# Reordering the prologue of a fused attention and token-mixer kernel, moving layernorm products to GpSimd, and telling its scheduler when the PV bank comes free

## Chip, cores and metric

The kernel runs on 1 core of one Trainium2 chip. The metric is the device time of one execution in microseconds (us); times are medians of 4 to 8 runs (two for `after_filler`, one for `forms`). A profile is one profiled execution, and its span is about 2 us shorter than its time. The engines are PE (TensorE; PEld is its weight load), ACT (ScalarE), DVE (VectorE), POOL (GpSimd) and SP (SyncE), which issues most DMAs here.

A ratio is of one kernel's runs to the other's of the same rounds. It is not the ratio of the medians quoted beside it, and differs from it by up to 0.15%. Different rounds ran on different chips; across rounds, the ratios compare better than the times.

## The reference

```
x = A_x                                   # 1 x 2048 x 512, bf16
xn = layernorm(x)                         # over the last axis, no weights
# A: attention, 32 heads of 16
q, k, v = split(xn @ wqkv)
oA = softmax(q k^T / 4) v  @ wo
# B: MLP over the token axis
h = layernorm(xn)
u = gelu(einsum("bsd,sf->bdf", h, w1) + b1)           # f = 1376
oB = transpose(einsum("bdf,fs->bds", u, w2) + b2)
out = x + oA + oB
```

## The kernel before

All instructions are generated by a Python program. For each engine it keeps a modelled clock and gives each instruction a cost. A prologue and attention block 0 (16 periods of two score tiles each) have a fixed order. The other 31 blocks are ordered by a greedy scheduler: at each step it takes the candidate that its model says can start first. Each engine gets its own list in that order; semaphores carry the dependences. So nothing on the chip waits for a modelled time; it decides the order.

A score tile of 128x1024 is exponentiated by ACT, or by DVE in a form of its own ("dexp", followed by three shifts on DVE or POOL). By the page of this kernel one took 1.14 to 1.15 us on ACT (L640), a dexp 1.22 us on DVE (L651), and a shift 0.45 us on DVE or 1.05 us on POOL (L656), all means. There are 1024 such tiles, called exps below, 32 to a block. "PV" is the product of probabilities and V, collected in one PSUM bank for a whole block. At the block's end DVE copies that bank out into OT.

The parts that matter:

```python
# prologue: memsets on POOL, the last of them
sc.add("pool", lambda e: e.memset(wo_t[:], 0.0), writes=[("wo_t", z) for z in range(4)], cost=(0.5, 0.6))
...
def late_consts():                    # called after block 0
    ... dma("sp", wo_c[...], ...)     # 8 loads
    ... dma("sp", wo_t[...], ...)     # 4 loads, after the wo_t memset
...
def ln_stats(t):                      # DVE bn_stats, bn_aggr; then POOL: (var + eps) ** -0.5
    ...
def ln_norm(t):
    sc.add("dve", lambda e: e.tensor_scalar(xn_sb[:, t, :], x_sb[:, t, :], mv[:, t, 0:1], mv[:, t, 2:3],
                                            ALU.subtract, ALU.mult), ...)
...
def pro_stage(s_, pre):               # one stage of the pipeline; period p of block 0 is stage p + 6
    # s_-5: evacuate K and V;  s_-4: K, (Q), V matmuls;  s_-3: copy xnT;  s_-2: transposes
    t = s_
    if ...: ln_stats(t)               # statistics first,
    t = s_ - 1
    if ...: ln_norm(t)                # then the product of the tile before it
...
for period in range(NKT):             # block 0
    # two score tiles and their exps on ACT; from period 2 on PV of two earlier ones
    block0_work(period)
late_consts()
for ft in range(NW): w1_load(ft)
...
# in the scheduler: PV is offered when its inputs are ready
jobs.append((max(t_c, a[0]), 0 if low else 2, "pv", a[1], 0.107))
```

The softmax here doesn't subtract the row's maximum and nothing guards it: scores larger than these inputs give would overflow.

## Time and profile before

| | before |
|---|---|
| time, median of 4 | 749.58 us (749.19 to 751.36) |
| ACT / PE / DVE / POOL busy | 95% / 92% / 86% / 47% |
| end of the 1st, 32nd, 1024th exp | 16.5, 47.9, 732.9 us |
| from the 32nd exp to the end of the span | 702.5 us |
| exps on DVE | 266 of 1024 |
| TensorE clock at half | 48.7 us of the span |

The exp times are the ends of exp instructions of the trace, put in order over ACT and DVE. The half-clock time is the sum of the clock's records in the trace, cut at the end of the span.

Three lines of the page: busy time by engine, and ACT and the granted TensorE clock in 40 slices of the span, in tenths.

```profile
PE 691.1 (92%) x12388; PEld 306.2 (41%) x12388; DVE 644.6 (86%) x1061; ACT 710.8 (95%) x779; POOL 351.5 (47%) x391
...
ACT  4899999999999999999999999989989999999990
...
PEclk9899999999999999999999999978989999999897
```

ACT is at 8 or 9 tenths from the second slice to the last but one, so time is to be had where ACT waits: at the start, and where the clock dips. The timeline of the start (start us, duration us, engine, line, operation, count, and in brackets the idle time before and what ended it):

```profile
4.16 1.80 POOL L400 MEMSET wo_t<- 128x2048 bf16 x1
...
6.04 0.23 POOL L456 TENSOR_SCALAR mv<-mv 128x1 f32<-128x1 f32 x1
...
6.35 0.57 POOL L458 TENSOR_TENSOR mv<-mv,mhalf 128x1 f32<-128x1 f32 x1
...
6.96 0.41 DVE L462 TENSOR_SCALAR hx<-x_sb,mv 128x512 bf16<-128x512 bf16 x1 [1.85 <-POOL mv L458]
...
14.25 0.69 ACT L553 ACTIVATE QT<-ps,qmask 128x512 bf16<-128x512 f32 x1 [0.60 <-PE ps L547]
...
15.43 5.75 ACT L640 ACTIVATE pT<-ps 128x1024 bf16<-128x1024 f32 x6 [0.32 <-PE ps L616]
```

POOL's memsets hold up the first rstd, and with it the first layernorm product (L462). The first exp starts at 15.43 us.

The waits over the span (who waited for whom: us in total, times, longest):

```profile
DVE pT L651 <- PE ps L616: 41.4, 50, 2.9
...
DVE x_sb L651 <- PE ps L616: 15.4, 17, 3.4
...
PE ps L679 <- DVE OT L863: 13.3, 26, 1.3
ACT pT L640 <- PE ps L616: 9.7, 15, 1.3
```

PE waits 26 times for the PV bank to be copied out; DVE waits 57 us for scores to exponentiate, and ACT 9.7. A line of the groups in the first 40 us (busy us, mean ns of one):

```profile
L531 POOL TENSOR_SCALAR VM<-V 128x544 bf16<-128x544 bf16 x3 | 1.9, 649 | 0.3
```

This is V times a constant, of about the product's size, in 0.65 us.

### The profile page before, as it was taken

How to read it: one execution, taken by the hardware profiler on the slowest of the kernel's cores; microseconds unless marked ns; L12 is line 12 of the kernel's file. 1: busy time of each engine (PE TensorE's matmuls, PEld its weight loads, DVE VectorE, ACT ScalarE, POOL GpSimd, SP SyncE). 2: the span in 40 equal slices, each digit the busy share in tenths (PEclk: the TensorE clock that was granted, in tenths of full speed). 3: DMA queues.
4: the chain of work that ended last, by engine and by line, in shares of the span. 5: the costliest groups of instructions: out<-in, count | busy, mean ns of one | idle time of the engine just before them, and what ended most of it. 6: DMA issues, size and time to landing. Idle time of an engine off the chain costs nothing.

```text
span 750.4 us, 28208 instructions
## 1 busy us (share of the span) xinstructions
PE 691.1 (92%) x12388; PEld 306.2 (41%) x12388; DVE 644.6 (86%) x1061; ACT 710.8 (95%) x779; POOL 351.5 (47%) x391
## 2 busy tenths in 40 slices
PE   4989999999999999999889999989899999989995
PEld 3544444444444434443333444333333444434332
DVE  6857788988999898899889988987979989999885
ACT  4899999999999999999999999989989999999990
POOL 6448355533434244355545435453454536446451
PEclk9899999999999999999999999978989999999897
DMA  7400000133233222210001222100001122111020
GB/s 206 84 3 24 18 13 17 23 73 72 47 69 65 62 49 51 54 43 21 23 15 31 50 51 61 36 15 16 23 16 29 47 51 52 38 31 36 17 58 29
DMA packets 85691, 32.25 MB, mean 43 GB/s; under 512 B 67392, under 2 KB 85568, under 8 KB 85568
## 3 DMA queue, kind: packets, MB, share of 16 engines
q1 hardware_dynamic: 82400, 28.87, 16.6%
q8 instruction: 97, 1.59, 0.9%
q10 hardware_dynamic: 3168, 1.57, 0.7%
q14 instruction: 26, 0.21, 0.1%
HBM read 21.76 MB, written 2.35 MB: 32 GB/s over the span
## 4 chain that ended last, share of the span: by engine, by line
ACT 41%; PE 31%; DVE 20%; POOL 3%; issue 2%; SPq 2%; DMA 0%; DVEq 0%; POOLq 0%
ACT pT L640 29%; PE ps L679 13%; ACT x_sb L640 12%; PE ps L616 11%; DVE pT L651 7%; PE ps L709 7%; DVE pT L656 5%; DVE x_sb L651 3%; SPq L371 2%; DVE OT L863 2%; DVE x_sb L656 1%; POOL pT L656 1%; POOL x_sb L656 1%; PE ps L758 1%; DVE denb L928 0%
## 5 line engine op out<-in xcount | busy, mean ns | idle before, releaser
L640 ACT ACTIVATE pT<-ps 128x1024 bf16<-128x1024 f32 x529 | 527.2, 1142 | 10.4 <-PE ps L616 9.7
L616 PE MATMUL ps<-QT,KT 32*128 32x512 bf16 x2048 | 285.1, 392 | 19.3 <-ACT pT L640 9.2
L651 DVE TENSOR_SCALAR pT<-ps 128x1024 int16<-128x1024 f32 x197 | 240.4, 1220 | 42.7 <-PE ps L616 41.4
L679 PE MATMUL ps<-pT,V 128*32 128x256 bf16 x4456 | 243.7, 282 | 13.6 <-DVE OT L863 7.0
L640 ACT ACTIVATE x_sb<-ps 128x1024 bf16<-128x1024 f32 x229 | 248.4, 1153 | 1.9 <-PE ps L616 1.9
L656 POOL TENSOR_SCALAR pT<-pT 128x1024 int16<-128x1024 int16 x137 | 143.5, 1047 | 175.6 <-DVE pT L656 125.1
L616 PEld LDWEIGHTS ps<-QT,KT 32*128 32x128 bf16 x2048 | 78.0, 91 | 194.4 <-ACT pT L640 80.7
L679 PEld LDWEIGHTS ps<-pT,V 128*32 128x32 bf16 x4456 | 106.0, 97 | 115.1 <-issue 72.5
L679 PE MATMUL ps<-x_sb,V 128*32 128x256 bf16 x1768 | 117.5, 282 | 9.0 <-DVE OT L863 6.3
L656 DVE TENSOR_SCALAR pT<-pT 128x1024 int16<-128x1024 int16 x288 | 120.8, 445 | 2.6
L656 POOL TENSOR_SCALAR x_sb<-pT 128x1024 int16<-128x1024 int16 x64 | 67.0, 1046 | 66.9 <-DVE pT L656 50.1
L651 DVE TENSOR_SCALAR x_sb<-ps 128x1024 int16<-128x1024 f32 x69 | 84.2, 1220 | 16.0 <-PE ps L616 15.4
L656 POOL TENSOR_SCALAR pT<-x_sb 128x1024 int16<-128x1024 int16 x53 | 55.4, 1046 | 63.2 <-DVE pT L656 46.1
L679 PEld LDWEIGHTS ps<-x_sb,V 128*32 128x32 bf16 x1768 | 45.5, 97 | 55.4 <-issue 32.8
L679 PE MATMUL ps<-pT,VM 128*32 128x256 bf16 x772 | 55.6, 278 | 0.4 <-POOL VM L531 0.3
L709 PE MATMUL ps<-hx,wblk 128*32 128x512 bf16 x688 | 52.8, 381 | 0.0
L656 DVE TENSOR_SCALAR x_sb<-pT 128x1024 int16<-128x1024 int16 x102 | 45.6, 453 | 0.8
L656 DVE TENSOR_SCALAR pT<-x_sb 128x1024 int16<-128x1024 int16 x103 | 43.5, 447 | 1.1
L709 PE MATMUL ps<-wkv_raw,wblk 128*32 128x512 bf16 x512 | 41.8, 381 | 0.4 <-DMA wblk<-in_B_w_dram 0.3
L900 POOL TENSOR_TENSOR oT<-oC,denb 128x256 bf16<-128x256 f32 (+1 forms) x32 | 23.3, 729 | 26.2 <-DVE pT L656 14.9
L656 POOL TENSOR_SCALAR x_sb<-x_sb 128x1024 int16<-128x1024 int16 x17 | 17.8, 1046 | 17.0 <-DVE pT L656 12.4
L679 PEld LDWEIGHTS ps<-pT,VM 128*32 128x32 bf16 x772 | 20.7, 97 | 10.2 <-issue 3.6
(85 smaller groups left out, 439.9 us busy)
## 6 DMA issues: line engine op xcount, KB each, us to landing
wblk<-in_B_w_dram SPq DMA_DIRECT2D x10, 512.0 KB, 5.2
wblk<-in_B_w_dram SPq DMA_DIRECT2D x16, 320.0 KB, 3.6
oC<-OT SPq DMA_DIRECT2D x248, 16.0 KB, 1.8
denb<-rden_scratch SPq DMA_DIRECT2D x124, 32.0 KB, 1.9
xr<-in_A_x_dram SPq DMA_DIRECT2D x16, 128.0 KB, 2.4
out_dram<-osb SPq DMA_DIRECT2D x16, 128.0 KB, 1.9
dcomp<-OT SPq DMA_DIRECT2D x124, 2.0 KB, 1.7
QT<-Qall SPq DMA_DIRECT2D x120, 16.0 KB, 1.8
```

The costliest lines, as they stand in the source:

```text
L371: return eng.dma_start(dst, src)
L616: specs.append(dict(eng="pe", fn=lambda e, r=r, bk=bk: e.matmul(bank(bk), lhsT=KT[32 * r:32 * r + 32, T, 128 * kt:128 * (kt + 1)], rhs=QT[ ...
L640: return [dict(eng="act", fn=lambda e: e.activation(buf(pbuf[n]), ps[:, s_ * 1024:(s_ + 1) * 1024], ACTF.Exp, scale=LN2_128), reads=[("ban ...
L651: return dict(eng="dve", fn=lambda e: e.tensor_scalar(buf_i(w), ps[:, s_ * 1024:(s_ + 1) * 1024], IBIAS, 0.0, ALU.add, ALU.max), reads=[(" ...
L656: return dict(eng=eng, fn=lambda e: e.tensor_scalar(buf_i(o), buf_i(w), float(SHIFTS[k]), 1.0, ALU.add, ALU.mult), reads=[("pT", w)], writ ...
L679: specs.append(dict(eng="pe", fn=lambda e, c=c, h=h, i=i, off=off: e.matmul(bank(PV_BANK)[32 * c:32 * c + 32, 256 * par:256 * par + 256], ...
L709: specs.append(dict(eng="pe", fn=lambda e, c=c, w=w: e.matmul(bank(EX_BANK)[32 * c:32 * c + w, :], lhsT=lhs_of(32 * c, 32 * c + w), rhs=rh ...
L758: specs.append(dict(eng="pe", fn=lambda e, ct=ct, c=c, i=i, t=t: e.matmul(bank(EX_BANK)[32 * c:32 * c + 32, 128 * i:128 * (i + 1)], lhsT=x ...
L863: yield "pvev", [dict(eng="dve", fn=lambda e: e.tensor_copy(OT32[:, eb, :], bank(PV_BANK)), reads=[("bank", PV_BANK)], writes=[("OT32", eb)])]
L900: yield "pool", [dict(eng="pool", fn=lambda e, cs=cs: e.tensor_tensor(oT[0:m, qb % 2, T, cs], oC32[0:m, tb_, cs], denb[0:m, tb_, cs], ALU. ...
```

## The change

Its intent is an earlier first exp, a lighter DVE in block 0, and a scheduler that doesn't park PE at an occupied bank. The diff, cut to its core (cuts marked "..."; modelled costs of memsets and of small matmuls were touched up, and the memsets of VM, QT and the ones in V moved or changed engine as well):

```diff
-        ld_w(2, 0, 1)  ... (all weights on the ACT queue, x on SP)
+        ld_x("sp", 0, 1)
+        ld_x("act", 1, 2)
+        ld_x("sp", 2, 3)
+        ld_x("act", 3, 4)
+        ... (then weights and the rest of x, all on SP)

-        sc.add("pool", lambda e: e.memset(wo_t[:], 0.0), ..., cost=(0.5, 0.6))      # in the prologue
         def late_consts():
+            sc.add("pool", lambda e: e.memset(wo_t[:], 0.0), ..., cost=(1.75, 1.8))

-        def ln_norm(t):
-            sc.add("dve", ...
+        def ln_norm(t, eng="pool"):
+            sc.add(eng, lambda e: e.tensor_scalar(xn_sb[:, t, :], x_sb[:, t, :], mv[:, t, 0:1], mv[:, t, 2:3],
                                                     ALU.subtract, ALU.mult),
-                   ..., cost=(0.3, 0.39))
+                   ..., cost=(0.3, 0.39) if eng == "dve" else (0.67, 0.75))

+        def ln_sums(t):      # ACT: Identity and Square with accumulated sums
+        def ln_moments(t):   # DVE: three operations on 128x1 make mean and variance of them
+        def warm_up(n):      # n matmuls of zeros, 128x512
+        ...
+        ln_sums(1)
+        warm_up(N_WARM)      # 11
+        ... statistics of tiles 0, 2, 3 on DVE, products of tiles 0 to 3 on DVE ...
+        ... transposes, copies, Q and K of tiles 0 to 3; Q evacuated in halves; V put off to period 0 ...

+        def block0_work(period):
+            ...
+            t = period + 5
+            if NPRE < t < NT:
+                ln_norm(t)           # on GpSimd, and ahead of the statistics
+            t = period + 6
+            if t < NT:
+                ln_stats(t)

-   jobs.append((max(t_c, a[0]), 0 if low else 2, "pv", a[1], 0.107))
+   jobs.append((max(t_c, a[0], sc.ready("pe", [], [("bank", PV_BANK)])), 0 if low else 2, "pv", a[1], 0.107))
```

More of the change, by code (lines that the diff above doesn't have):

```diff
@@ L47 @@
 NPRE = 4
+N_WARM = 11
 SEM = 0.05
@@ L342, in bass_parallel_sum__softmax_full_mha__mixer_token_mlp__prompt_kernel @@
         osb = sb("osb", [128, 2, 512], BF16)
+        warm = osb[:, 0, :]
         rden_d = nc.dram_tensor("rden_scratch", [2, 2048], F32, kind="Internal").ap()
@@ L372, in dma @@
             return sc.add(q, fn, reads=reads, writes=writes, name=name, dma=True, out_dma=out_dma)
-        sc.add("pool", lambda e: e.memset(ident[:], 0.0), writes=[("ident",)])
+        sc.add("pool", lambda e: e.memset(ident[:], 0.0), writes=[("ident",)], cost=(0.25, 0.3))
         sc.add("pool", lambda e: e.affine_select(ident[:], ident[:], [[-1, 128]], ALU.not_equal, 1.0,
                                                  base=0, channel_multiplier=1),
-               reads=[("ident",)], writes=[("ident",)])
-        sc.add("pool", lambda e: e.memset(mhalf[:], -0.5), writes=[("mhalf",)])
-        sc.add("dve", lambda e: e.memset(b1c_bf[:], 0.0), writes=[("b1c",)])
+               reads=[("ident",)], writes=[("ident",)], cost=(0.4, 0.5))
+        sc.add("pool", lambda e: e.memset(mhalf[:], -0.5), writes=[("mhalf",)], cost=(0.1, 0.2))
+        sc.add("dve", lambda e: e.memset(warm, 0.0), writes=[("warm",), ("osb", 0)], cost=(0.06, 0.1))
+        sc.add("dve", lambda e: e.memset(b1c_bf[:], 0.0), writes=[("b1c",)], cost=(0.06, 0.1))
         v17_main = V17[:, 0:NKT * H * 17].rearrange("p (n c) -> p n c", c=17)
@@ L387, in bass_parallel_sum__softmax_full_mha__mixer_token_mlp__prompt_kernel, with late_memsets, ld_x @@
         sc.add("dve", lambda e: e.memset(V17[:, NKT * H * 17:], 0.0), writes=[("V", NKT, 0)], cost=(0.06, 0.1))
-        sc.add("dve", lambda e: e.memset(v17_main[:, :, 16:17], 0.5), writes=[("Vone",)], cost=(0.4, 0.5))
-        sc.add("pool", lambda e: e.memset(qmask[:, 0:1], 0.0), writes=[("qmask",)])
+        sc.add("pool", lambda e: e.memset(qmask[:, 0:1], 0.0), writes=[("qmask",)], cost=(0.1, 0.2))
         for r in range(4):
             sc.add("pool", lambda e, r=r: e.memset(qmask[32 * r:32 * r + 16, 0:1], QSCALE),
-                   reads=[("qmask",)], writes=[("qmask",)])
+                   reads=[("qmask",)], writes=[("qmask",)], cost=(0.15, 0.2))
         sc.add("pool", lambda e: e.tensor_scalar(qmask[:, 1:2], qmask[:, 0:1], -1.0, QSCALE, ALU.mult, ALU.add),
-               reads=[("qmask",)], writes=[("qmask",)])
-        for T in range(1, 4):
-            sc.add("pool", lambda e, T=T: e.memset(vm_kh[:, :, 8 * T, 0:16], 0.0),
-                   writes=[("VM", t, T) for t in range(NT)], cost=(0.3, 0.4))
-        sc.add("pool", lambda e: e.memset(VM[:, NKT * H * 17:], 0.0), writes=[("VM", NKT, 0)], cost=(0.1, 0.2))
-        sc.add("pool", lambda e: e.memset(QT[:, 2:4, :], 0.0), writes=[("QT", i, r) for i in (2, 3) for r in range(4)], cost=(0.9, 1.0))
-        sc.add("pool", lambda e: e.memset(wo_t[:], 0.0), writes=[("wo_t", z) for z in range(4)], cost=(0.5, 0.6))
-        def ld_x(a, b_):
-            dma("sp", x_sb[:, a:b_, :],
+               reads=[("qmask",)], writes=[("qmask",)], cost=(0.2, 0.25))
+        def late_memsets():
+            for T in range(1, 4):
+                sc.add("pool", lambda e, T=T: e.memset(vm_kh[:, :, 8 * T, 0:16], 0.0),
+                       writes=[("VM", t, T) for t in range(NT)], cost=(0.3, 0.4))
+            sc.add("pool", lambda e: e.memset(VM[:, NKT * H * 17:], 0.0), writes=[("VM", NKT, 0)], cost=(0.1, 0.2))
+        def ld_x(q, a, b_):
+            dma(q, x_sb[:, a:b_, :],
                 x2[128 * a:128 * b_, :].rearrange("(t p) d -> p t d", p=128),
@@ L414, in ld_w @@
                 keys = [("wkv", j - 1, T) for T in range(T0_, T1_)]
-            dma("act", dst, A_wqkv[:, c0:c1].rearrange("(ct p) n -> p ct n", p=128),
+            dma("sp", dst, A_wqkv[:, c0:c1].rearrange("(ct p) n -> p ct n", p=128),
                 reads=[], writes=keys, name="ld_wqkv")
-        ld_w(2, 0, 1)
-        ld_w(1, 0, 1)
-        ld_w(0, 0, 1)
-        ld_w(1, 1, 4)
-        ld_w(2, 1, 4)
-        ld_w(0, 1, 4)
-        ld_x(0, 1)
-        ld_x(1, 2)
-        ld_x(2, 4)
-        ld_x(4, 8)
-        ld_x(8, 12)
-        ld_x(12, 16)
+        ld_x("sp", 0, 1)
+        ld_x("act", 1, 2)
+        ld_x("sp", 2, 3)
+        ld_x("act", 3, 4)
+        for j in (1, 0, 2):
+            ld_w(j, 0, 1)
+        ld_x("sp", 4, 6)
+        ld_x("sp", 6, 8)
+        ld_x("sp", 8, 12)
+        ld_x("sp", 12, 16)
+        for j in (1, 2, 0):
+            ld_w(j, 1, 4)
         NFTF = F // 128
@@ L437, in late_consts @@
         def late_consts():
+            sc.add("pool", lambda e: e.memset(wo_t[:], 0.0), writes=[("wo_t", z) for z in range(4)], cost=(1.75, 1.8))
             for e_ in range(2):
@@ L455, in ln_stats @@
                    reads=[("stats", t)], writes=[("mv", t)], cost=(0.12, 0.18))
-            sc.add("pool", lambda e: e.tensor_scalar(mv[:, t, 3:4], mv[:, t, 1:2], EPS, None, ALU.add),
-                   reads=[("mv", t)], writes=[("mv", t)], cost=(0.2, 0.28))
-            sc.add("pool", lambda e: e.tensor_tensor(mv[:, t, 2:3], mv[:, t, 3:4], mhalf[:], ALU.pow),
-                   reads=[("mv", t), ("mhalf",)], writes=[("mv", t)], cost=(0.5, 0.57))
-        def ln_norm(t):
-            sc.add("dve", lambda e: e.tensor_scalar(xn_sb[:, t, :], x_sb[:, t, :], mv[:, t, 0:1], mv[:, t, 2:3],
+            ln_rstd(t, 1)
@@ new lines, in ln_rstd @@
+        def ln_rstd(t, n):
+            mk = [("mv", t + i) for i in range(n)]
+            sc.add("pool", lambda e: e.tensor_scalar(mv[:, t:t + n, 3], mv[:, t:t + n, 1], EPS, None, ALU.add),
+                   reads=mk, writes=mk, cost=(0.2, 0.28))
+            sc.add("pool", lambda e: e.tensor_tensor(mv[:, t:t + n, 2], mv[:, t:t + n, 3], mhalf[:].to_broadcast([128, n]), ALU.pow),
+                   reads=mk + [("mhalf",)], writes=mk, cost=(0.5, 0.57))
+        def ln_sums(t):
+            for fn, col in ((ACTF.Identity, 3), (ACTF.Square, 1)):
+                sc.add("act", lambda e, fn=fn, col=col: e.activation(xn_sb[:, t, :], x_sb[:, t, :], fn,
+                                                                    accum_out=mv[:, t, col:col + 1]),
+                       reads=[("x", t)], writes=[("xn", t), ("mv", t)], cost=(0.55, 0.7))
@@ new lines, in ln_moments @@
+        def ln_moments(t):
+            sc.add("dve", lambda e: e.tensor_scalar(mv[:, t, 0:1], mv[:, t, 3:4], 1.0 / D, None, ALU.mult),
+                   reads=[("mv", t)], writes=[("mv", t)], cost=(0.07, 0.12))
+            sc.add("dve", lambda e: e.tensor_tensor(mv[:, t, 3:4], mv[:, t, 0:1], mv[:, t, 0:1], ALU.mult),
+                   reads=[("mv", t)], writes=[("mv", t)], cost=(0.07, 0.12))
+            sc.add("dve", lambda e: e.scalar_tensor_tensor(mv[:, t, 1:2], mv[:, t, 1:2], 1.0 / D, mv[:, t, 3:4],
+                                                           ALU.mult, ALU.subtract),
+                   reads=[("mv", t)], writes=[("mv", t)], cost=(0.07, 0.12))
@@ L463, in ln_norm @@
+        def ln_norm(t, eng="pool"):
+            sc.add(eng, lambda e: e.tensor_scalar(xn_sb[:, t, :], x_sb[:, t, :], mv[:, t, 0:1], mv[:, t, 2:3],
                                                     ALU.subtract, ALU.mult),
-                   reads=[("x", t), ("mv", t)], writes=[("xn", t)], cost=(0.3, 0.39))
+                   reads=[("x", t), ("mv", t)], writes=[("xn", t)], cost=(0.3, 0.39) if eng == "dve" else (0.67, 0.75))
         def ln2_stats():
@@ L492, in transpose_pe @@
                     xn_sb[:, t, ct * 128:(ct + 1) * 128], ident[:]),
-                    reads=[("xn", t), ("ident",)], writes=[("bank", bk)], cost=("F", (0, 1, 2, 3), 0.08))
+                    reads=[("xn", t), ("ident",)], writes=[("bank", bk)], cost=("F", (0, 1, 2, 3), 0.06))
         def transpose_copy(t, bk, eng):
@@ L505, in kt_tile_pe @@
                     rhs=xnT[:, ct, 128 * t:128 * (t + 1)], start=(ct == 0), stop=(ct == NCT - 1)),
-                    reads=[("wkv", 0, T), ("xnT", t)], writes=[("bank", bk)], cost=("F", (0, 1, 2, 3), 0.08))
+                    reads=[("wkv", 0, T), ("xnT", t)], writes=[("bank", bk)], cost=("F", (0, 1, 2, 3), 0.06))
         def kt_tile_evac(T, t, bk, evac_eng):
@@ L518, in vt_tile_pe @@
                     start=(ct == 0), stop=(ct == NCT - 1)),
-                    reads=[("wkv", 1, T), ("xnT", t)], writes=[("bank", bk)], cost=("F", (0, 1, 2, 3), 0.08))
+                    reads=[("wkv", 1, T), ("xnT", t)], writes=[("bank", bk)], cost=("F", (0, 1, 2, 3), 0.06))
         def vt_evac(tiles, T, bk, evac_eng):
@@ L534, in vm_scale @@
                 cost=(0.62, 0.7))
-        def tb(t):
-            return t % 2 if t < NPRE else 4
-        def vb(t):
-            return 2 + (t % 2) if t < NPRE else 5
-        def kb(t):
-            return PV_BANK if t < NPRE else EX_BANK
+        QB = (EX_BANK, 4)
         def qt0_tile_pe(t):
+            bk = QB[t // 2]
             for ct in range(NCT):
                 sc.add("pe", lambda e, ct=ct: e.matmul(
-                    bank(EX_BANK)[:, 128 * t:128 * (t + 1)], lhsT=wq_sb[:, ct, 0:128],
+                    bank(bk)[:, 128 * t:128 * (t + 1)], lhsT=wq_sb[:, ct, 0:128],
@@ L549, in qt0_tile_pe @@
                     rhs=xnT[:, ct, 128 * t:128 * (t + 1)], start=(ct == 0), stop=(ct == NCT - 1)),
-                    reads=[("wq", 0), ("xnT", t)], writes=[("bank", EX_BANK)], cost=("F", (0, 1, 2, 3), 0.08))
-        def qt0_evac():
-            sc.add("act", lambda e: e.activation(QT[:, 0, :], bank(EX_BANK), ACTF.Identity, scale=qmask[:, 0:1]),
-                   reads=[("bank", EX_BANK), ("qmask",)], writes=[("QT", 0, r) for r in range(4)], cost=(0.6, 0.69))
-            sc.add("dve", lambda e: e.tensor_scalar(QT[:, 1, :], bank(EX_BANK), qmask[:, 1:2], None, ALU.mult),
-                   reads=[("bank", EX_BANK), ("qmask",)], writes=[("QT", 1, r) for r in range(4)])
@@ L558, in pro_stage @@
-        def pro_stage(s_, pre):
-            ev = "act" if pre else "dve"
-            last = NPRE if pre else NT
-            def ok(t):
-                return (0 if pre else NPRE) <= t < last
-            t = s_ - 5
-            if ok(t):
-                if t == NPRE - 1:
-                    qt0_evac()
-                kt_tile_evac(0, t, kb(t), "dve" if t >= NPRE else ("dve" if t % 2 == 0 else "act"))
-                vt_evac([t], 0, vb(t), ev if t % 2 == 0 else "dve")
-            t = s_ - 4
-            if ok(t):
-                kt_tile_pe(0, t, kb(t))
-                if t < NPRE:
-                    qt0_tile_pe(t)
-                vt_tile_pe(t, 0, vb(t), 0)
-            t = s_ - 3
-            if ok(t):
-                transpose_copy(t, tb(t), ev)
-            t = s_ - 2
-            if ok(t):
-                transpose_pe(t, tb(t))
-            t = s_
-            if (0 if pre else NPRE + 2) <= t < (NPRE + 2 if pre else NT):
-                ln_stats(t)
-            t = s_ - 1
-            if (0 if pre else NPRE + 2) <= t < (NPRE + 2 if pre else NT):
-                ln_norm(t)
@@ L590, in bass_parallel_sum__softmax_full_mha__mixer_token_mlp__prompt_kernel, with qt0_evac @@
-        NSTG_PRE = NPRE + 5
-        for s_ in range(NSTG_PRE):
-            pro_stage(s_, True)
-        def block0_work(period):
-            pro_stage(period + NPRE + 2, False)
+                    reads=[("wq", 0), ("xnT", t)], writes=[("bank", bk)], cost=("F", (0, 1, 2, 3), 0.06))
+        def qt0_evac(half, eng):
+            cs = slice(256 * half, 256 * half + 256)
+            src = bank(QB[half])[:, cs]
+            rd, wr = [("bank", QB[half]), ("qmask",)], [("QT", 0, r) for r in range(4)]
+            if eng == "act":
+                sc.add("act", lambda e: e.activation(QT[:, 0, cs], src, ACTF.Identity, scale=qmask[:, 0:1]),
+                       reads=rd, writes=wr, cost=(0.4, 0.5))
+            else:
+                sc.add("dve", lambda e: e.tensor_scalar(QT[:, 0, cs], src, qmask[:, 0:1], None, ALU.mult),
+                       reads=rd, writes=wr, cost=(0.35, 0.42))
@@ new lines, in warm_up @@
+        def warm_up(n):
+            for _ in range(n):
+                sc.add("pe", lambda e: e.matmul(bank(5), lhsT=warm[:, 0:128], rhs=warm, start=True, stop=True),
+                       reads=[("warm",)], writes=[("bank", 5)], cost=("F", (0, 1, 2, 3), 0.3), name="warm")
+        sc.add("act", lambda e: e.activation(rcomp[:, 0, 0:1], mhalf[:], ACTF.Exp), reads=[("mhalf",)],
+               writes=[("rcomp", 0)], cost=(1.4, 1.5))
+        ln_sums(1)
+        warm_up(N_WARM)
+        sc.add("pool", lambda e: e.memset(v17_main[:, :, 16:17], 0.5), writes=[("Vone",)], cost=(0.5, 0.6))
@@ new lines, in bass_parallel_sum__softmax_full_mha__mixer_token_mlp__prompt_kernel @@
+        ln_stats(0)
+        sc.add("dve", lambda e: e.bn_stats(stats[:, 2, :], x_sb[:, 2, :]), reads=[("x", 2)], writes=[("stats", 2)], cost=(0.6, 0.69))
+        sc.add("dve", lambda e: e.bn_aggr(mv[:, 2, 0:2], stats[:, 2, :]), reads=[("stats", 2)], writes=[("mv", 2)], cost=(0.12, 0.18))
+        ln_moments(1)
+        ln_rstd(1, 2)
+        ln_stats(3)
+        for t in range(NPRE):
+            ln_norm(t, "dve")
+        late_memsets()
+        TB = (0, 1, 2, 3)
+        for t in range(NPRE):
+            transpose_pe(t, TB[t])
@@ new lines, in bass_parallel_sum__softmax_full_mha__mixer_token_mlp__prompt_kernel @@
+        for t in range(NPRE):
+            transpose_copy(t, TB[t], "dve" if t == 2 else "act")
+        for t in range(NPRE):
+            qt0_tile_pe(t)
+            if t == 0:
+                kt_tile_pe(0, t, PV_BANK)
+                kt_tile_evac(0, t, PV_BANK, "dve")
+            if t == 1:
+                qt0_evac(0, "dve")
+        for t in range(1, NPRE):
+            kt_tile_pe(0, t, PV_BANK)
+        qt0_evac(1, "act")
+        ln_stats(NPRE)
+        for half in range(2):
+            cs = slice(256 * half, 256 * half + 256)
+            sc.add("dve", lambda e, half=half, cs=cs: e.tensor_scalar(QT[:, 1, cs], bank(QB[half])[:, cs], qmask[:, 1:2], None, ALU.mult),
+                   reads=[("bank", QB[half]), ("qmask",)], writes=[("QT", 1, r) for r in range(4)], cost=(0.35, 0.42))
@@ new lines, in bass_parallel_sum__softmax_full_mha__mixer_token_mlp__prompt_kernel @@
+        evac("dve", KT[:, 0, 128:512], bank(PV_BANK)[:, 128:512], reads=[("bank", PV_BANK)],
+             writes=[("KTt", 0, t) for t in range(1, NPRE)], cost=(0.45, 0.52))
+        ln_norm(NPRE)
+        ln_stats(NPRE + 1)
+        def block0_work(period):
+            if period == 0:
+                for t in range(NPRE):
+                    vt_tile_pe(t, 0, 5, t)
+                vt_evac(list(range(NPRE)), 0, 5, "dve")
+            t = period + 1
+            if NPRE <= t < NT:
+                kt_tile_evac(0, t, EX_BANK, "dve")
+                vt_evac([t], 0, 5, "dve")
+            t = period + 2
+            if NPRE <= t < NT:
+                kt_tile_pe(0, t, EX_BANK)
+                vt_tile_pe(t, 0, 5, 0)
+            t = period + 3
+            if NPRE <= t < NT:
+                transpose_copy(t, 4, "dve")
+            t = period + 4
+            if NPRE <= t < NT:
+                transpose_pe(t, 4)
+            t = period + 5
[3 more added lines that the diff above has]
+            if t < NT:
+                ln_stats(t)
+            if period == 1:
+                sc.add("pool", lambda e: e.memset(QT[:, 2:4, :], 0.0),
+                       writes=[("QT", i, r) for i in (2, 3) for r in range(4)], cost=(0.9, 1.0))
```

## The prediction

> **What bounds the kernel.** From 48 to 732 us it exponentiates score tiles on ScalarE, with VectorE taking about a quarter (groups: 758 and 266 exps). ACT is busy 95% of the span. Its idle time (waits, and busy time by window): 15.4 us before the first exp, 1.9 us in block 0, 9.4 us of waits for scores from 48 to 735 us, and the tail. Nearly all waits in between fall where the granted TensorE clock is 0.5 (19.0 to 25.6, 371 to 374, 497 to 508, around 520, 545 to 552, 693 to 698 us). Elsewhere ACT is full: only moving tiles to DVE helps.
>
> **Prologue, from the timeline.** x0 is usable by 3.24 us, but GpSimd is in memsets (the last, wo_t, 1.80 us) until 6.0, so the first rstd (0.23 + 0.57 us) frees the first layernorm product only at 6.96. Then DVE alternates statistics (0.69 + 0.18) and products (0.4) for six tiles, and evacuates; the Q evacuation (0.69) ends at 14.94, and the first exp starts at 15.43.
>
> The change takes the GpSimd block, statistics of tiles 4 and 5, V and the 512-wide Q evacuation out of that chain. My estimate after: x0 at 3.1 (issue 0.7, plus 2.4 as a 128 KB load takes later); DVE statistics of 0 and 2, three small moment operations, statistics of 3 until 6.3; products until 7.9, the last waiting for GpSimd; transposes until 8.4; ACT copies 3 x 0.6 until 9.05; Q matmuls until 9.5; half Q evacuation until 10.0; first exp at **10.5 us** (9.7 to 12). Gain: 4.9 us, all critical. No second table load: before, one serves Identity, Exp and Tanh[...].
>
> **Block 0.** Exps run every 0.958 us except for bubbles of 1.35 and 0.55 us while the clock was 0.5. PE was mostly 40 to 67% busy from 14 to 19 us, then the clock dropped. [...]here matmuls sped up at 12.2, 5 us after PE's first. The 11 zero matmuls should have PE fast at the transposes, and four V tiles fill period 0. An even chance that the bubbles go: gain 1.0. Products on GpSimd (0.67 each; VM's similar 128x544 took 0.65) free 0.35 of DVE's 1.93 us period, but ACT's pace of 1.92 hides it.
>
> **PV bank.** PE waits 13.3 us, 26 times, for the OT copy releasing it. Scores can now go first. ACT does not wait for them, but DVE waits 57 us for scores, so more tiles go to DVE. I expect 2.5 us, 0 to 5. The schedule is greedy, so later choices shift: clock dips, worth 7.5 us of ACT waits, may multiply or vanish (plus or minus 4).
>
> **Sum:** 749.6 - 4.9 - 1.0 - 2.5 = **741.2 us**, range 735.5 to 747. Faster by over 2% 0.09, within 2% 0.90, slower 0.01.
>
> **Checks.** First exp near 10.5 in the timeline, one table load; clock not 0.5 in the first 25 us; the 32nd exp ending near 42, not 48; PE's wait for the OT copy under 5 us; over 266 DVE exps; from there to the end 699, not 702.
>
> **What would make it wrong.** x later[...]; an ACT accumulation slower than 0.7 us; GpSimd late with products in block 0; new half-clock stretches.

That only one table load would come had one observation behind it, the single load of the kernel before (1.28 us at 4.00 us), which serves its Identity, Exp and Tanh; Square is new in the change. That the zero matmuls would have PE fast at the transposes had one too, the matmuls that sped up at 12.2 us (four of 128x128 took 0.63 us before, 0.39 after). The 0.7 us for an ACT accumulation is the limit, with no source given; in the trace of the change one took 0.63 us and reading its sum 0.19 (L471).

## The result, and the profile after

| | before | after |
|---|---|---|
| time, median of 4 | 749.58 us | 769.75 us (768.85 to 770.45) |
| ratio | | 1.0254, 95% interval 1.023 to 1.0279 |
| end of the 1st, 32nd, 1024th exp | 16.5, 47.9, 732.9 us | 12.4, 60.0, 748.3 us |
| from the 32nd exp to the end of the span | 702.5 us | 708.5 us |
| exps on DVE | 266 | 269 |
| TensorE clock at half | 48.7 us | 106.4 us |

The change is slower by 2.5%. In the profiled spans (750.4 and 768.5 us) the 18.1 us are made up thus: 4.1 won at the first exp, 16.2 lost between the first and the 32nd exp, and 6.0 lost after it. (By the medians the loss is 20.2 us: the profiled execution before was a slower one than the median, judging by its span.) The same lines of the page:

```profile
PE 709.6 (92%) x12435; PEld 310.9 (40%) x12435; DVE 644.4 (84%) x1055; ACT 709.2 (92%) x776; POOL 385.1 (50%) x411
...
ACT  4569999999999999899999999999999999999990
...
PEclk9559999999999999998989999988989999979998
```

ACT is now at 5 and 6 tenths, and the clock at 5, in the second and third slices: block 0. The timeline of the start:

```profile
10.44 0.47 ACT L574 ACTIVATE QT<-ps,qmask 128x256 bf16<-128x256 f32 x1 [0.66 <-DVE QT L577]
...
11.40 1.94 ACT L696 ACTIVATE pT<-ps 128x1024 bf16<-128x1024 f32 x2 [0.48 <-PE ps L672]
...
12.24 2.09 POOL L485 TENSOR_SCALAR hx<-x_sb,mv 128x512 bf16<-128x512 bf16 x1
...
14.47 0.38 PE L513 MATMUL ps<-ident,hx 128*128 128x128 bf16 x4 [2.11 <-POOL hx L485]
...
14.79 0.40 PE L672 MATMUL ps<-QT,KT 32*128 32x512 bf16 x4
...
15.22 1.94 ACT L696 ACTIVATE pT<-ps 128x1024 bf16<-128x1024 f32 x2 [1.88 <-PE ps L672]
...
15.28 2.08 POOL L485 TENSOR_SCALAR hx<-x_sb,mv 128x512 bf16<-128x512 bf16 x1
```

The first exp starts 4.0 us earlier, at 11.40. Then one GpSimd product takes 2.09 us. The transposes (L513) of that tile wait for it. The next scores (L672), which come after the transposes in PE's list, start at 14.79, behind the transposes of 14.47, although ACT had ended its exps at 13.34; and ACT waits 1.88 us for the scores. The instructions of line L485, with minimum, median and maximum in ns, one row for each engine:

```profile
L485 POOL TENSOR_SCALAR hx<-x_sb,mv x12: 2084/2090/2091, 12.2 to 48.1; 128x512 bf16<-128x512 bf16 x12
L485 DVE TENSOR_SCALAR hx<-x_sb,mv x4: 381/410/868, 6.5 to 7.8; 128x512 bf16<-128x512 bf16 x4
```

The duration doesn't scatter: 2.09 us every time. The chain that ended last, from 12 to 52 us, by line:

```profile
by line: POOL hx L485 62.7%; POOL mv L465 17.2%; issue 5.9%; POOL mv L463 5.7%; POOL VM L554 3.2%; POOL QT L651 2.2%; PE ps L513 1.5%; PE ps L672 1.4%; PE ps L735 1.4%
```

GpSimd alone makes up nine tenths of the chain (91%); the product and the rstd before it are 86%. Per tile that is 0.23 + 0.57 + 2.09 us and gaps, 3.04 us for two exps where the kernel before took 1.92. The waits that answer to those of before:

```profile
DVE pT L707 <- PE ps L672: 38.5, 48, 1.6
ACT pT L696 <- PE ps L672: 28.4, 29, 3.8
...
DVE x_sb L707 <- PE ps L672: 15.9, 17, 3.5
...
PE ps L735 <- DVE OT L919: 2.2, 7, 0.6
```

The wait for the PV bank nearly vanished, as predicted (that of PE's weight loads for the same copy fell from 24.3 to 8.2 us), and DVE's wait for scores stayed. ACT's wait for scores rose by 18.7 us. Last, the part of the change that looked harmless. The SP queue's timeline before, and after:

```profile
16.44 3.71 SPq L371 DMA_DIRECT2D wo_c<-in_A_wo_dram  x8
20.19 2.80 SPq L371 DMA_DIRECT2D wo_t<-in_A_wo_dram  x4
```

```profile
16.77 3.71 SPq L373 DMA_DIRECT2D wo_c<-in_A_wo_dram  x8
58.57 1.92 SPq L373 DMA_DIRECT2D wo_t<-in_A_wo_dram  x4
```

The wo_t loads wait for the memset, the memset now waits behind block 0's work on POOL, and SP's queue issues nothing in between: 38 us of standstill in the change (20.48 to 58.57 us). The loads of wblk, which follow in its list, were issued at 60.5 us instead of 23.0.

### The profile page after: what moved, and what is told of

The parts are those of the page before. It is cut to its first block, busy times and chain, and to the rows that moved or that the text cites. A ratio compares the mean times of both kernels' runs of the same rounds, so it can differ in the third digit from the quotient of the medians.

```text
span 768.5 us, 28346 instructions
## 1 busy us (share of the span) xinstructions
PE 709.6 (92%) x12435; PEld 310.9 (40%) x12435; DVE 644.4 (84%) x1055; ACT 709.2 (92%) x776; POOL 385.1 (50%) x411
## 4 chain that ended last, share of the span: by engine, by line
ACT 58%; PE 19%; DVE 12%; POOL 7%; DMA 1%; issue 1%; SPq 0%; POOLq 0%; DVEq 0%
ACT pT L696 43%; ACT x_sb L696 15%; PE ps L735 7%; PE ps L672 7%; DVE pT L707 4%; PE ps L765 4%; POOL hx L485 3%; DVE pT L712 2%; DVE x_sb L707 1%; POOL mv L465 1%; POOL pT L712 1%; DVE x_sb L712 1%; DVE OT L919 1%; DMA rden_scratch<-rcomp 1%; DVE denb L984 0%
## 5 line engine op out<-in xcount | busy, mean ns | idle before, releaser
L696 ACT ACTIVATE pT<-ps 128x1024 bf16<-128x1024 f32 x563 | 555.7, 1137 | 29.2 <-PE ps L672 28.4
L672 PE MATMUL ps<-QT,KT 32*128 32x512 bf16 x2048 | 286.3, 404 | 22.0 <-ACT pT L696 10.5
L735 PE MATMUL ps<-pT,V 128*32 128x256 bf16 x4516 | 255.5, 288 | 5.1 <-DVE OT L919 2.0
L707 DVE TENSOR_SCALAR pT<-ps 128x1024 int16<-128x1024 f32 x181 | 220.6, 1219 | 39.1 <-PE ps L672 38.5
L696 ACT ACTIVATE x_sb<-ps 128x1024 bf16<-128x1024 f32 x192 | 210.9, 1145 | 4.0 <-PE ps L672 3.7
L672 PEld LDWEIGHTS ps<-QT,KT 32*128 32x128 bf16 x2048 | 76.5, 91 | 198.4 <-ACT pT L696 84.0
L707 DVE TENSOR_SCALAR x_sb<-ps 128x1024 int16<-128x1024 f32 x88 | 107.2, 1219 | 16.3 <-PE ps L672 15.9
L712 DVE TENSOR_SCALAR pT<-pT 128x1024 int16<-128x1024 int16 x250 | 105.1, 443 | 2.2
L712 POOL TENSOR_SCALAR pT<-x_sb 128x1024 int16<-128x1024 int16 x62 | 64.7, 1043 | 75.0 <-DVE pT L712 56.6
L712 POOL TENSOR_SCALAR x_sb<-pT 128x1024 int16<-128x1024 int16 x57 | 59.5, 1043 | 56.1 <-DVE pT L712 36.9
L712 DVE TENSOR_SCALAR pT<-x_sb 128x1024 int16<-128x1024 int16 x132 | 56.8, 451 | 1.4
L712 POOL TENSOR_SCALAR x_sb<-x_sb 128x1024 int16<-128x1024 int16 x28 | 29.2, 1043 | 32.1 <-DVE pT L712 25.3
```

What stands on the lines that cost most here:

```text
L672: specs.append(dict(eng="pe", fn=lambda e, r=r, bk=bk: e.matmul(bank(bk), lhsT=KT[32 * r:32 * r + 32, T, 128 * kt:128 * (kt + 1)], rhs=QT[ ...
L696: return [dict(eng="act", fn=lambda e: e.activation(buf(pbuf[n]), ps[:, s_ * 1024:(s_ + 1) * 1024], ACTF.Exp, scale=LN2_128), reads=[("ban ...
L707: return dict(eng="dve", fn=lambda e: e.tensor_scalar(buf_i(w), ps[:, s_ * 1024:(s_ + 1) * 1024], IBIAS, 0.0, ALU.add, ALU.max), reads=[(" ...
L712: return dict(eng=eng, fn=lambda e: e.tensor_scalar(buf_i(o), buf_i(w), float(SHIFTS[k]), 1.0, ALU.add, ALU.mult), reads=[("pT", w)], writ ...
L735: specs.append(dict(eng="pe", fn=lambda e, c=c, h=h, i=i, off=off: e.matmul(bank(PV_BANK)[32 * c:32 * c + 32, 256 * par:256 * par + 256], ...
```

## The experiments

Three theories for the loss came up, and the runs tell them apart:

- Theory 1: the 2.09 us product on GpSimd paces block 0.
- Theory 2: the half clock, brought about by the new prologue, paces block 0.
- Theory 3 (formed after the first eight runs): the loss after block 0 comes from the moved wo_t memset.

All runs, with the kernel before of the same rounds beside them:

| run | what it is | median us | before us | ratio | 32nd exp us | from there to the end us |
|---|---|---|---|---|---|---|
| after | the change | 769.75 | 749.58 | 1.0254 | 60.0 | 708.5 |
| dve_prod | change, products on DVE | 757.37 | 750.39 | 1.0094 | 48.1 | 706.4 |
| pv_only | before + PV knowledge | 746.43 | 750.39 | 0.9936 | 48.3 | 695.9 |
| forms | six forms of the product (wrong result) | 762.41 | 750.39 | | 53.7 | 706.9 |
| after_filler | change + zero matmuls in block 0 | 760.92 | 750.39 | 1.0133 | 58.4 | 701.0 |
| pool_madd | change, product as multiply-add | 756.63 | 749.70 | 1.0086 | 48.7 | 706.2 |
| dve_order | dve_prod, statistics first | 752.88 | 749.70 | 1.0034 | 43.7 | 707.3 |
| dve_prod_nopv | dve_prod without PV knowledge | 763.26 | 749.70 | 1.0179 | 48.1 | 713.1 |
| model_true | change, scheduler told 2.09 us | 771.18 | 749.70 | 1.0291 | 59.8 | 706.4 |
| order_wot | dve_order, wo_t memset early | 744.21 | 751.04 | 0.9912 | 44.8 | 700.2 |
| order_hidden | order_wot, memset really late | 744.65 | 751.04 | 0.9918 | 44.7 | 701.0 |
| after_wot | change, wo_t memset early | 761.52 | 751.04 | 1.0144 | 60.8 | 702.4 |
| before_wotlate | before, wo_t memset late | 761.94 | 751.04 | 1.0132 | 49.0 | 711.8 |
| pool_prod_only | before, GpSimd products | 760.44 | 750.88 | 1.0121 | 57.7 | 700.6 |
| order_nowarm | order_wot without zero matmuls | 744.11 | 750.88 | 0.9902 | 44.8 | 697.0 |

All but `forms` gave correct results. The 95% intervals of the ratios reach 0.23 to 0.5% to either side. The last two columns come from one profiled run each, and are good to about 3 us: that run was the slowest of its four in order_wot, after_wot, order_hidden and before_wotlate (3.0, 3.5, 3.0 and 1.0 us above the median), and the fastest in model_true (3.2 below).

### 1. Products back on DVE

```diff
-                ln_norm(t)            # block 0
+                ln_norm(t, "dve")
-        ln_norm(NPRE)                 # end of the prologue
+        ln_norm(NPRE, "dve")
```

> The changed kernel with the layernorm products of tiles 4 to 15 back on VectorE, nothing else undone. Theory 1 (the GpSimd product, 2.09 us in the trace of the change, paces block 0): first exp stays near 12.4 us at its end, exps then follow every 0.96 us, the 32nd ends near 43 us instead of 60.0, the half-clock stretch from 17 to 61 us shrinks to a few us or goes, total near 748 us if the later blocks keep the 3 us they lost, 745 if not. Theory 2 (the half clock itself, brought by the new prologue, paces block 0): the 32nd exp still ends after 55 us and the clock stays at 0.5.

Block 0 recovered 11.9 us and the half clock in it shrank to two stretches of 3.4 us (and one at its end), so theory 2 fails and theory 1 gains. But the 32nd exp ended at 48.1, not 43: the head start of 4 us was lost again within block 0. The trace shows DVE waiting 0.3 to 0.7 us in each period for the rstd of the tile it wants to multiply, since the new order puts the product ahead of the statistics. That is tested in run 6.

### 2. The PV knowledge alone

```diff
-   jobs.append((max(t_c, a[0]), 0 if low else 2, "pv", a[1], 0.107))
+   jobs.append((max(t_c, a[0], sc.ready("pe", [], [("bank", PV_BANK)])), 0 if low else 2, "pv", a[1], 0.107))
```

> The kernel before with only the scheduler's knowledge of the PV bank's release added. The prediction's theory (DVE gets scores earlier): 747 us, 745 to 749. Rival (the change reshuffles a greedy schedule and the wait was harmless): within 1 us either way of 749.6, PE's wait for the OT copy down from 13.3 to about 2 us, DVE exps within 5 of 266.

It gains 0.64% (95% interval of the ratio 0.991 to 0.9961), 4 us by the medians. The prediction had 2.5. PE's wait for the copy falls from 13.3 to 2.8 us. The route is not the one that the prediction named: DVE exps rose by two only, to 268. What fell is the half clock, from 48.7 to 40.1 us, and ACT's wait for scores, from 11.6 to 6.1 us (into pT and x_sb together), a wait that the prediction had not expected to change here. Why these fell is not shown.

### 3. What a GpSimd product costs, by form

```diff
+            if eng == "pool":
+                s1, s2, o1, o2 = (
+                    (mean, rstd, subtract, mult),  # tiles 4, 10: as in the change
+                    (mean, 1.0, subtract, mult),   # 5, 11
+                    (rstd, 1.0, mult, mult),       # 6, 12
+                    (rstd, mean, mult, add),       # 7, 13
+                    (0.0, 1.0, subtract, mult),    # 8, 14
+                    (0.0, rstd, subtract, mult))[(t - NPRE) % 6]   # 9, 15
```

(written here with short names)

> A wrong result on purpose. The changed kernel with the GpSimd product of the 12 tiles of block 0 in six forms, two tiles each: both operands per-partition columns with subtract then multiply; subtract a column then times 1.0; multiply a column then times 1.0; multiply a column then add a column; two constants; a constant then a column. If two column operands are what costs: 2.09 us in the first and fourth, about 0.69 in the others. If the subtract costs: 2.09 in the first, second, fifth and sixth, 0.69 in the third and fourth. If contention with VectorE costs: durations scatter, whatever the form.

The first six products in POOL's timeline, tiles 4 to 9 in order:

```profile
12.04 2.09 POOL L494 TENSOR_SCALAR hx<-x_sb,mv 128x512 bf16<-128x512 bf16 x1
...
15.08 2.02 POOL L494 TENSOR_SCALAR hx<-x_sb,mv 128x512 bf16<-128x512 bf16 x1
...
18.15 0.69 POOL L494 TENSOR_SCALAR hx<-x_sb,mv 128x512 bf16<-128x512 bf16 x1
...
20.70 0.76 POOL L494 TENSOR_SCALAR hx<-x_sb,mv 128x512 bf16<-128x512 bf16 x1
...
23.09 1.94 POOL L494 TENSOR_SCALAR hx<-x_sb 128x512 bf16<-128x512 bf16 x1
...
26.11 2.01 POOL L494 TENSOR_SCALAR hx<-x_sb,mv 128x512 bf16<-128x512 bf16 x1
```

All four forms that begin with subtract took 1.94 to 2.09 us, even with two constants; multiply-multiply took 0.69 and multiply-add with two columns 0.76. Each column operand adds 0.07 (1.94, 2.01 or 2.02, and 2.09 us with none, one and two). The second six tiles repeat these durations to 0.01 us. So it is the operations (subtract, then multiply), not the columns; and of contention with VectorE, which the expectation took to scatter the durations, these show no sign. Whether subtract is slow in every pairing is not shown; add first was not tried on bf16, but the shifts on POOL (L656 of the kernel before: add, then multiply, constants, int16) took 1.05 us for 128x1024, twice the elements. The prediction had priced a subtract by the duration of a multiply.

### 4. The clock held up in block 0

```diff
             if NPRE <= t < NT:
+                warm_up(6)            # 6 zero matmuls of 512 columns
                 transpose_pe(t, 4)
```

(V tiles moved into the K tiles' bank, so that one bank is free for the zeros.)

> The changed kernel with its GpSimd products, but six more zero matmuls of 512 columns ahead of each tile's transposes in block 0, to hold the TensorE clock up (the V tiles share the K tiles' bank to free one). Theory 1: the clock stays at 1.0, yet block 0 keeps its period of about 3.04 us per two exps and the 32nd exp ends at 58 to 62 us. Theory 2: with the clock at 1.0 the period falls to about 2 us and the 32nd exp ends near 46 us.

Two stretches of 3 us in the change, then the same two with the fillers (stretch: its length, busy us and count of PE, PEld, DVE, ACT and POOL, then granted clock, DMA share and GB/s):

```profile
29.00:32.00 3.00, 2.49 (x28) 1.37 (x24) 1.64 (x6) 1.94 (x2) 2.85 (x3) 0.50 0.01 3
38.00:41.00 3.00, 2.60 (x28) 1.33 (x24) 1.79 (x5) 1.94 (x2) 2.81 (x4) 0.50 0.00 0
```

```profile
29.00:32.00 3.00, 2.73 (x30) 1.33 (x30) 1.51 (x6) 1.78 (x3) 2.81 (x4) 1.00 0.01 3
38.00:41.00 3.00, 2.85 (x37) 1.41 (x30) 1.63 (x7) 1.90 (x3) 2.85 (x3) 1.00 0.00 0
```

The clock was full until 55.8 us, and yet ACT was busy for 1.8 to 1.9 us of 3, as before, and POOL for 2.8. The 32nd exp came only 1.6 us earlier. So the half clock in block 0 of the change is not the cause of its pace. With more work on PE (2.73 and 2.85 us busy of 3, against 2.49 and 2.60) the clock stayed full, though the pace was the same. The total fell by 8.8 us all the same, 7.5 of it after block 0 by the profiles: the fillers moved the modelled times, and the scheduler made another order. That was the hint that the later blocks had a loss of their own.

### 5. The product in its fast form

```diff
+  mv[:, t, 3] = mean * rstd * -1.0                # one more 128x1 operation on GpSimd
-  xn = (x - mean) * rstd
+  xn = x * rstd + mv[:, t, 3]
```

> The changed kernel with the GpSimd product written as x times rstd plus a column, the column (minus mean times rstd) made by one more tiny GpSimd operation. If the slow thing is subtract on GpSimd, the product takes 0.76 us as in the run of six forms, GpSimd needs about 0.22 + 0.57 + 0.22 + 0.76 and gaps, 2.1 us per tile instead of 3.0, and the 32nd exp ends at 46 to 49 us instead of 60.0. With 688 us from there on, as in the change, and the tail included in the total: 756 us, 752 to 760.

It came out as expected: the product takes 0.77 us, the 32nd exp ends at 48.7, the total is 756.63. With the two 0.57 and 0.22 operations of rstd and the one more of 0.27, GpSimd needs 2.20 us per tile with its gaps (14.62 to 16.82 us in the timeline), still a little more than ACT's 1.92, so this is no better than DVE.

### 6. Statistics before the product

```diff
-            t = period + 5: ln_norm(t, "dve")
             t = period + 6: ln_stats(t)
+            t = period + 5: ln_norm(t, "dve")
```

> Products on VectorE, and in each period the statistics of the next tile before the product, the order of the kernel before. Theory: VectorE's waits of 0.3 to 0.7 us for GpSimd's rstd in each period, seen in the run with products on VectorE, go, and the 32nd exp ends at 44 to 46 us instead of 48.1; total 752 to 756. Rival: those waits are hidden, and the 32nd exp stays near 48 us.

The 32nd exp ended at 43.7 us, so the head start is now kept: 4.2 us ahead of the kernel before. The total is 752.88, still 0.3% slower than before. All that is lost is now behind block 0: 707.3 us against 702.5.

### 7. Is it the PV knowledge that costs later?

```diff
-   jobs.append((max(t_c, a[0], sc.ready("pe", [], [("bank", PV_BANK)])), ...
+   jobs.append((max(t_c, a[0]), ...
```

> Products on VectorE and the scheduler again without the knowledge of the PV bank's release. If that knowledge is worth the 4 us it gave alone, this is slower than with it: about 761 us. If its worth depends on the schedule it meets: anything from 750 to 764, with PE's wait for the OT copy back at about 13 us, and the 32nd exp at 48 us either way.

No: without it the kernel is 5.9 us slower (763.26 against 757.37 for dve_prod), and PE's wait for the copy is back at 15.4 us. The knowledge is worth 4 to 6 us in both settings.

### 8. Is it the wrong number in the scheduler's table?

```diff
-   cost=(0.3, 0.39) if eng == "dve" else (0.67, 0.75))
+   cost=(0.3, 0.39) if eng == "dve" else (2.09, 2.17))
```

> The changed kernel with one number different: the scheduler's table says 2.09 us for the GpSimd product instead of 0.67. The instructions of block 0 stay in their order, so the 32nd exp still ends at 60 us. Theory: a wrong number in the table makes the later schedule bad; then the time from the 32nd exp to the end falls from 708 to about 702 us or less. Rival: later choices just shift with any number, and it changes by up to 6 us either way.

No gain: 771.18 us, and 706.4 from the 32nd exp on against 708.5, in the fastest of its four runs. So correcting the table was not what the later blocks lacked; the 702 us or less of that theory did not come.

### 9. The wo_t memset back in the prologue

Of the eight kernels run so far with the new prologue and its late memset, seven needed 706 to 713 us from the 32nd exp to the end; the eighth, after_filler, 701.0; so the loss does not come with every order that has the late memset. A late memset has this in the scheduler's own modelled clock (not on the chip): SP's queue is taken until 45 us, where in the old kernel it is free at 16. Four runs tested it together:

```diff
# order_wot and after_wot: out of late_consts(), into the prologue's POOL memsets
# before_wotlate: the reverse, in the kernel before
 def late_consts():
-    sc.add("pool", lambda e: e.memset(wo_t[:], 0.0), ..., cost=(1.75, 1.8))
# order_hidden: the memset stays in late_consts(), and the model is told otherwise
+    late = sc.add("pool", lambda e: e.memset(wo_t[:], 0.0), ...)
+    late.t1, sc.free["pool"], sc.port_free["pool"] = 5.0, free_, port_
```

> Products on VectorE after the statistics, and the wo_t memset (1.80 us on GpSimd) back in the prologue, before block 0, instead of after it. Theory 3 (that memset's move is what made the later blocks slow, because the DMA queue that waits for it stands still through block 0 and the greedy schedule that follows is another one): the time from the 32nd exp to the end falls from 707 to about 696 us, as in the run with the PV knowledge alone, and the total to 742 us, 739 to 745. Rival (later differences are luck of the schedule, unrelated to the memset): 748 to 757.

> The change with only the wo_t memset put back before block 0; GpSimd products stay. Theory 3: the 32nd exp still ends at 60 us, the rest takes about 696 to 700 instead of 708 us, total 757 to 761. Rival: total within 3 us of 769.75.

> The kernel before with only the wo_t memset moved behind block 0. Theory 3: exps of block 0 as before (the 32nd at 48 us), the rest about 10 us longer, total 757 to 762 us. Rival: within 4 us of 749.6.

> The instructions of the run order_wot, in the same order on every engine, except that the wo_t memset really runs after block 0 and the scheduler is told it was done at 5 us. If what costs is the DMA queue really standing still: slower than order_wot by up to 10 us, near 752. If it is only the schedule that the scheduler makes when it believes the queue stands still: within 2 us of order_wot.

Theory 3 holds in all four, though three sizes were missed by a little: after_wot took 761.52 us (757 to 761 expected), with 702.4 after block 0 (696 to 700), and order_wot's 700.2 after block 0 were 4 more than expected, with its total of 744.21 inside the 739 to 745. Both profiled runs were the slowest of their four, by about as much as the later blocks missed. Moving the memset back took 8.7 us off dve_order and 8.2 off the change; moving it late in the kernel before cost 10.9. And order_hidden, whose instruction lists equal order_wot's on every engine but for the place of that one memset, has the same time, 744.65 against 744.21. Its SP queue did stand still, as this line of its waits shows (us, times, longest):

```profile
SPq L373 <- POOL mv L495: 22.8, 1, 22.8
```

So the standstill itself costs nothing measurable. What costs is the order that the scheduler makes when it believes in it. How that order loses time can be seen in parts only. In dve_prod, ACT waits 3.75 us at one place (305.9 to 309.6 us) for scores, at the start of block 12, while PE runs PV matmuls and those of the MLP's second product; order_wot and the kernel before have no such wait. And the clock's half-rate stretches come in other places. In the kernel before, the four blocks in which PE has no side work, no projection or MLP matmul, hold 27.8 of its 48.7 us at half clock.

A two-by-two of the time from the 32nd exp to the end fits this, within those 3 us: 702.5 us with neither, 695.9 with the PV knowledge and 711.8 with the late memset, all in the kernel before; with both, 706 to 709, but in the new prologue (after_filler's 701.0 apart), where the PV knowledge without the late memset gave 697.0 to 702.4 and the late memset without the knowledge 713.1.

### 10. The two remaining questions

The GpSimd product alone, in the kernel before:

```diff
-                ln_norm(t)
+                ln_norm(t, "dve" if pre else "pool")     # pro_stage; tiles 6 to 15 on GpSimd
```

> The kernel before with only the layernorm products of tiles 6 to 15 moved to GpSimd (subtract, then multiply, as in the change; the scheduler is told 0.67 us, as in the change). Theory 1: each such period becomes 3.0 us or more, and the ten products add about 10 x 1.1 = 11 us: the 32nd exp ends at 58 to 62 us instead of 47.9, total 758 to 764. Rival (GpSimd is only slow together with the new prologue and the half clock it brings): total within 4 us of 750.

It costs 9.6 us by the medians, with the 32nd exp at 57.7, 9.8 us late and just short of the 58 to 62 expected. The time from the 32nd exp on did not suffer (700.6). The line of its ten products:

```profile
L462 POOL TENSOR_SCALAR hx<-x_sb,mv x10: 2084/2094/2095, 19.2 to 46.5; 128x512 bf16<-128x512 bf16 x10
```

A half-clock stretch of 23.9 us (27.1 to 51.0) came with them, without the new prologue. Theory 1 needs nothing else of the change.

The zero matmuls:

```diff
-N_WARM = 11
+N_WARM = 0
```

> The run order_wot without the 11 zero matmuls; everything else in the same order. If they warm the clock as the prediction says: the transposes, K and Q matmuls run at half speed, and the first exp ends about 1 us later than 12.2. If TensorE is not on that path: within 0.3 us of 12.2. The later clock drop at about 17 us stays in both cases. Total 743 to 747.

The timeline's line of the Q matmuls of tiles 1 to 3, first without the zeros (order_nowarm), then with them (order_wot):

```profile
9.99 1.23 PE L564 MATMUL ps<-xnT,wq_sb 128*128 128x128 bf16 x12
```

```profile
9.22 0.83 PE L564 MATMUL ps<-xnT,wq_sb 128*128 128x128 bf16 x12
```

The twelve matmuls take 1.23 us without the zeros and 0.83 with them. The trace's first clock record, of a full clock, starts at 10.8 us without the zeros and at 6.8 with them; before its first record the views print 1.00, which is no measurement (without the zeros also for 9 to 10 us, where four matmuls took 0.63 us, against 0.39 with them). The first exp ends at 13.3 instead of 12.2 us, so the zeros do have TensorE fast earlier. But the 32nd exp ends at 44.8 us in both, and the totals are 744.11 and 744.21: the microsecond is lost again in block 0, whose half clock lasted 6.8 us with the zeros and 3.4 without, in the profiled runs.

## Why the prediction was wrong

The time is 28.6 us above the 741.2 predicted. By the profile, 18 us of that stood at the 32nd exp (near 42 predicted, 60.0 measured), and 9.5 came after it (699 and 708.5).

- **First exp at 10.5 us (9.7 to 12).** Right, but by 0.9 us short of the gain: 11.40. The first statistics began at 3.52 instead of 3.1, and the last of the four products took 0.87 us instead of 0.4. One table load (1.28 us at 1.65 us), as predicted, with Square among the functions.
- **"Products on GpSimd (0.67 each; VM's similar 128x544 took 0.65)".** This is the step that failed. The line that it was priced by is a multiply by a constant; the product is a subtract and a multiply, 2.09 us each time. With it fell "ACT's pace of 1.92 hides it": GpSimd's 3.04 us per tile became the pace of block 0. "GpSimd late with products in block 0" stood on the prediction's own list of what would make it wrong, but without a size. Undone alone it gives back 12.4 us; done alone in the old kernel it costs 9.6.
- **An even chance that the bubbles and the half clock go.** They grew: block 0 had one half-clock stretch of 6.8 us (19.0 to 25.8) before, with another beginning at its end (46.3 to 49.7), and one of 44.4 us (17.0 to 61.3) after. The filler run shows that this was not the cause: with a full clock until 55.8 us, the 32nd exp still ended at 58.4, against 60.0.
- **PV bank: 2.5 us, 0 to 5.** The wait fell as said, and the gain was larger: 4.0 us alone, 5.9 within the new prologue. But the route was wrong: DVE took hardly more tiles, 268 against 266 in pv_only, while ACT, which "does not wait", waited 5.5 us less for scores. A gain within the forecast 0 to 5 does not confirm the route.
- **A term that was missing.** The moved wo_t memset was seen only as 1.8 us that leave the prologue. It costs 8 to 11 us, because of the order that the scheduler makes of it. "Later choices shift" had been allowed 4 us either way; that margin was too small. In each of the three pairs that differ by the memset's place the loss came back (8.2, 8.7 and 10.9 us); after_filler, with another order, went without it.
- **After block 0: 699 us predicted, 708.5 measured.** That is the PV knowledge's gain, outweighed by the memset's loss.

With those two terms taken out, order_wot, and order_nowarm without the zeros, run in 744 us (741.2 had been predicted), 0.9 to 1.0% faster than the kernel before, and so are faster than both kernels. Against pv_only (0.9936), their ratios of 0.9912 and 0.9902 come from other rounds; the intervals overlap. So it is not shown that the new prologue adds to the PV knowledge in the total, though its 32nd exp ends 3.5 us earlier (44.8 against 48.3). What stays open is how the PV knowledge gains its 4 us, and how the order after block 0 turns a believed standstill into 10 us; only two of its places were seen.

## What to carry to other kernels

Price an instruction by a line of the trace with the same engine and the same operations, not only the same shape: on GpSimd a product written as subtract and multiply took 2.7 times as long as the same product written as multiply and add (2.09 against 0.77 us). Where an order is made by a greedy model, each moved instruction, even one that no engine waits for, is a change of every later choice, so move one thing at a time and time it. If a clock or a busy share drops along with the time, hold it up artificially once, to see whether it is cause or consequence.

## What the traces show of the TensorE clock

- Half-clock stretches in the two kernels' records last 3.4 us or multiples of it (3.4, 6.8 and 10.2 us in both, and 44.4, 13 times 3.4, in the change), but for the last of each run (9.8 and 9.5 us), which the end of the records cuts. How busy PE must be for the clock to come back is not shown. In the change it stayed at half clock for 44 us while PE was busy for 61 to 88% of each stretch of 3 us from 17 to 53 us (1.82 to 2.65 of 3.00), and for all of one from 53 to 56 (3.00), without the clock coming back; it came back at 61.3 us, in a stretch (59 to 62) that was busy throughout.
- The slow start is not in the clock records: in the kernel before, the first record starts at 12.2 us, and the views print 1.00 for the time before it, although four 128x128 matmuls took 0.61 to 0.63 us until 11.5 us, as long as at 20.5 to 23.8 us, where the record says 0.50, and 0.39 from 12.3 us on. So it is a record missing here, not a wrong one.
